# Window attention feeding a gated FFN: softplus dummies, other homes for gated parts, seven half products in ten chunks instead of eleven, fewer fillers, a new written-out order

## The chip, the cores and the metric

One core of one Trainium2 chip. The metric is device time in microseconds of one execution. The kernel before takes 897.61 us as the median of three runs (897.12 to 897.76). Engine names are those of the profile: PE (TensorE matmul), PEld (its weight load), DVE (VectorE), ACT (ScalarE), POOL (GpSimd), SP (the DMA-issuing queue).

## The reference, cut to what matters

Eight batches of eight heads, 576 positions, head width 64. Then 4608 tokens go through an FFN with d_model 512 and d_ff 2048.

```python
scores = scale * q @ k.T                       # only 0 <= i - j < 64 is kept
attn = exp(scores - rowmax) ; attn /= attn.sum + 1e-9
x = (attn @ v)  reshaped to (4608, 512)
h = x @ w_in
sp = max(h, 0) + log1p(exp(-abs(h)))           # softplus
g = h * erf(sp)
out = g @ w_out                                # float32
```

The weights come as 64-bit floats; the chip unpacks them. Each float32 operand of a product is scaled and split into two float16 parts (hi, lo), and a product is hi·hi + hi·lo + lo·hi, so every multiplication costs three matmuls.

## The kernel before, in words

The 4608 tokens are 36 attention units `u` of 128 tokens, and 18 FFN chunks `c` of 256 tokens. A chunk's FFN has two halves of d_ff, so there are 36 groups `g`; from chunk 2 on, group g belongs to chunk g // 2.

There is no planner on the chip. `PLAN` is one long string of tokens such as `sp:35:1`; the loop at the end of the kernel calls a handler for each token in that order, and each handler issues its instructions at once. Each engine therefore runs its own instructions strictly in the order in which their tokens stand, and waits with semaphores for data of the others. A last letter names the engine where there is a choice: a ACT, v DVE, g POOL, d a DMA that POOL issues.

The tokens that the change and the prediction touch:

- `wm:n` issues n filler matmuls on PE that nothing reads (line 993).
- Attention of a unit: `s` scores on PE (505), `m` masked maximum on DVE (514), `f` subtract it, `e` the exponential on ACT (539), `ph` and `r` its hi and lo parts (577/579 and 546), `a` the product with v, `n` the normalization.
- First FFN product, chunks 4 to 17 (from `FIRST`): `M:g:m`, seven products m = 1, 2, 6, 5, 7, 4, 3 of 24 matmuls with 128 columns each (809), into two PSUM banks; `E` copies a bank out and `C` (825, DVE) adds the other bank to what was copied, into the buffer `hb[g % 2]`.
- Activation: `sp:g:n` softplus on ACT (833), `er:g:n` erf on ACT (837), `gt:g:n` the gate h · erf on DVE (842 from chunk `FAST` on, else 844). Exp, softplus and erf are in different activation tables, so ACT loads a table (`ACT_TABLE_LOAD`) wherever the kind changes.
- Second FFN product, below `FAST`: `gh` and `gl` split the gate into hi and lo, `mA` and `mB` multiply by w_out in 512-column matmuls (868; 96 of them for a chunk), `fo` takes the result out.
- Second FFN product, from `FAST` on: seven half products in the order `SERIES` = 1, 4, 2, 5, 6, 3, 7 as listed by number, run as 1, 4, 2, 5, 6, 7, 3 in the plan. `A` and `B` (577/579 and 933) make the hi and lo part of one quarter of the gate, held in `yb`, and put them into a place that `slot(c, m, h)` names; `P` and `Q` (954) multiply them, in 256-column matmuls (168 for a chunk); `S` adds one quarter to another for the later products; `O` clears a PSUM bank; `K` and `J` (420/422 and 971/974) take results out. The combined right-hand sides come from w_out through `Z`, `Yh`, `Yl`.

`slot` in the kernel before puts two products' parts in halves of `hb[1]`, the buffer of the odd groups; only products 1 and 7 of the last chunk (`NCH` - 1 = 17) go into `vr`, the buffers of the attention's v, which are free by then. `E` of group 35 writes `hb[1]`, so in program order it stands behind all `P` and `Q` of chunk 16.

`FAST` also sets `LONE` (how many units have doubled attention buffers) and `LENT` (from which chunk the gate's split uses `hb`).

Of the kernel before, what the change touches and what calls it, by code (L numbers as in the profile page):

```python
# [18 lines left out]
B, H, S, D = 8, 8, 576, 64  # L19
# [25 lines left out]
FAST = 7  # L45
# [246 lines left out]
def window_attention_gated_ffn(ctx, tc, q, k, v, w_in, w_out, masks, out):  # L292
# [538 lines left out]

    def softplus(g, n):
        nc.scalar.activation(at(yb, g, n), at(hb, g, n), AF.Softplus, scale=st_c[g][:, n:n + 1])  # L833

    def erf(g, n):
        y = at(yb, g, n)
        nc.scalar.activation(y, y, AF.Erf)  # L837
# [228 lines left out]
```

## Time and profile before

| what | value |
|---|---|
| median of three runs | 897.61 us |
| the profiled execution's own time | 895.71 us |
| its span, first to last instruction | 893.8 us |
| PE busy | 821.5 us (92%) |
| DVE busy | 787.4 us (88%) |
| ACT busy | 702.4 us (79%) |
| POOL busy | 406.2 us (45%) |
| mean granted TensorE clock | 0.990 |

The profile is of one execution. Engine names with a trailing q are the engine's sequencer, which waits. "busy" is the union of the instructions' own times; a matmul's end is modelled, so matmul rates are better read from starts of uniform runs of matmuls. In a chain of waits, each piece is the work that the next piece waited for, from the last instruction backwards. Lines such as L954 are lines of the kernel before.

### The profile page before, as it was taken

To read this page: it belongs to the slowest core of one execution; us is meant where nothing else is said; L and a number is where in the kernel's file an instruction comes from. 1 tells how busy PE (TensorE), PEld (TensorE's weight loads), DVE (VectorE), ACT (ScalarE), POOL (GpSimd) and SP (SyncE) were. 2 spreads that over 40 slices of the span, in tenths; PEclk is the share of its full clock that TensorE was granted. 3 is DMA by queue.
4 is the path that set the end of the run, shared out by engine and by line. 5 is a ranking of instruction groups with operands and counts; after the bars stand their busy time and mean duration, and the time that the engine had idled before them with its cause. 6 is when DMAs were issued, how large, how long until landed. Compare 5 with 4: busy or idle time off the path is not lost.

```text
span 893.8 us, 28169 instructions
## 1 busy us (share of the span) xinstructions
PE 821.5 (92%) x11952; PEld 679.9 (76%) x11952; DVE 787.4 (88%) x1680; ACT 702.4 (79%) x960; POOL 406.2 (45%) x384
## 2 busy tenths in 40 slices
PE   7989998999999989999889999899899998999977
PEld 6878766576676646678788878788789887889866
DVE  5799999999999989999999989898889898777845
ACT  3799989799999886979698869886779865765662
POOL 3253464431553336556473737553635352542332
PEclk9999999999999999999999999999999999999999
DMA  9963366434647354534557776793675733422100
GB/s 360 397 210 128 120 168 136 106 103 83 134 98 149 87 135 100 134 104 108 121 125 162 132 134 133 139 192 84 137 115 127 109 76 63 90 49 69 25 25 24
DMA packets 149101, 111.52 MB, mean 125 GB/s; under 512 B 123504, under 2 KB 123888, under 8 KB 148976
## 3 DMA queue, kind: packets, MB, share of 16 engines
q1 hardware_dynamic: 145808, 98.60, 45.4%
q0 software_dynamic: 3024, 11.01, 6.8%
q8 instruction: 93, 1.52, 0.7%
q14 instruction: 32, 0.26, 0.1%
q10 hardware_dynamic: 144, 0.13, 0.0%
HBM read 59.64 MB, written 9.44 MB: 77 GB/s over the span
## 4 chain that ended last, share of the span: by engine, by line
DVE 41%; PE 26%; ACT 21%; issue 9%; DMA 3%; POOL 1%; SPq 0%; DVEq 0%; ACTq 0%; POOLq 0%
PE o L954 9%; PE hp L809 8%; DVE h L933 5%; ACT y L833 4%; DVE sm L514 4%; DVE y L842 3%; ACT y L837 3%; DVE h L825 3%; ACT h L577 2%; ACT L833 2%; PE o L868 2%; DVE vs L427 2%; PE hp L765 2%; PE av L993 2%; ACT L837 2%
## 5 line engine op out<-in xcount | busy, mean ns | idle before, releaser
L954 PEld LDWEIGHTS <-h 128*128 128x128 f16 x1800 | 172.1, 98 | 52.7 <-ACT h L577 11.8
L809 PE MATMUL hp<-arena,w 128*128 128x128 f16 x2688 | 163.8, 219 | 5.4 <-DVE h L825 3.0
L809 PEld LDWEIGHTS <-w 128*128 128x128 f16 x2688 | 155.5, 98 | 12.5 <-issue 7.0
L954 PE MATMUL o<-w,h 128*128 128x256 f16 x1008 | 124.7, 276 | 16.1 <-ACT h L577 9.5
L809 PE MATMUL hp<-arena 128*128 128x128 f16 x2016 | 122.3, 220 | 12.6 <-ACT h L577 8.4
L809 PEld LDWEIGHTS <-arena 128*128 128x128 f16 x2016 | 116.1, 98 | 18.4 <-issue 15.2
L933 DVE TENSOR_TENSOR h<-y,h 128x512 f16<-128x512 f32 x107 | 89.2, 856 | 11.2 <-ACT h L577 6.0
L933 POOL TENSOR_TENSOR h<-y,h 128x512 f16<-128x512 f32 x43 | 57.4, 1339 | 73.3 <-ACT h L577 36.3
L765 PE MATMUL hp<-arena,w 128*128 128x256 f16 (+1 forms) x960 | 88.8, 252 | 1.7 <-ACT h L577 1.0
L833 ACT ACTIVATE y<-h,c 128x1024 f32<-128x1024 f32 x72 | 80.6, 1143 | 9.4 <-DVE h L825 7.1
L577 ACT ACTIVATE h<-y 128x512 f16<-128x512 f32 x101 | 59.4, 620 | 34.6 <-PE o L954 17.3
L765 PEld LDWEIGHTS <-w 128*128 128x128 f16 x960 | 77.4, 98 | 11.2 <-issue 2.1
L577 ACT ACTIVATE h<-hp 128x512 f32<-128x512 f32 x111 | 64.5, 583 | 19.1 <-PE hp L809 16.7
L868 PE MATMUL o<-w,gh 128*128 128x512 f16 x320 | 75.1, 379 | 1.1 <-DVE ob L982 1.1
L837 ACT ACTIVATE y<-y 128x1024 f32<-128x1024 f32 x72 | 74.8, 1051 | 0.4
L842 DVE SCALAR_TENSOR_TENSOR y<-h,small,y 128x1024 f32<-128x1024 f32 x44 | 57.4, 1316 | 19.6 <-ACT y L837 19.5
L825 DVE TENSOR_TENSOR h<-hp,h 128x512 f32<-128x512 f32 x84 | 57.4, 684 | 13.5 <-PE hp L809 10.9
L954 PE MATMUL o<-spare,h 128*128 128x256 f16 x506 | 62.0, 273 | 6.9 <-DVE ob L974 3.5
L833 ACT ACT_TABLE_LOAD x39 | 50.0, 1283 | 22.9 <-DVE h L825 14.9
L514 DVE CUSTOM_DVE_ANT_0 sm<-s,mask 128x128 f32<-128x128 f32 x268 | 60.9, 284 | 6.2 <-PE s L505 4.2
L519 POOL TENSOR_TENSOR sm<-sm,small 128x512 f32<-128x512 f32 x42 | 51.7, 1236 | 28.7 <-DVE small L514 22.1
L868 PEld LDWEIGHTS <-gh 128*128 128x128 f16 x320 | 30.5, 98 | 33.8 <-issue 1.4
(254 smaller groups left out, 1743.7 us busy)
## 6 DMA issues: line engine op xcount, KB each, us to landing
vr<-v_in SPq DMA_DIRECT2D x36, 520.0 KB, 4.1
kr<-k_in SPq DMA_DIRECT2D x36, 384.0 KB, 4.0
y<-y POOLq DMA_DIRECT2D x21, 512.0 KB, 4.9
qr<-q_in SPq DMA_DIRECT2D x36, 256.0 KB, 3.4
out<-ob SPq DMA_DIRECT2D x33, 256.0 KB, 2.4
arena<-w_in SPq DMA_DIRECT2D x4, 1024.0 KB, 8.6
w<-w_in SPq DMA_DIRECT2D x4, 1024.0 KB, 8.8
arena<-w_out SPq DMA_DIRECT2D x4, 1024.0 KB, 5.4
```

The costliest lines, as they stand in the source:

```text
L514: nc.vector.tensor_tensor_reduce(smi(u, par)[:, j, :], sps[par][:, j, :], mask[:, var, :], 1.0, LOWEST, op0=ALU.add, op1=ALU.max, accum_ou ...
L519: eng_of(eng).tensor_tensor(s, s, m.unsqueeze(2).broadcast_to([P, HP, P]), op=ALU.subtract)
L577: nc.scalar.activation(dst, src, AF.Copy)
L765: nc.tensor.matmul(hps[pc % 2][:, f, at_t], w1[a][hf][:, cc, fs], xt[b][c % 2][:, cc:2 * NCC:NCC, :][:, at_x, :], start=(n == 0), stop=(n ...
L809: nc.tensor.matmul(bank[:, q, f, :], left(m, a, 2 * hf + q)[:, cc, f * P:(f + 1) * P], xt[b][c % 2][:, slot + cc, :], start=m in (1, 2, 5) ...
L825: nc.vector.tensor_tensor(dst, bank_view(1), dst, op=ALU.add)
L833: nc.scalar.activation(at(yb, g, n), at(hb, g, n), AF.Softplus, scale=st_c[g][:, n:n + 1])
L837: nc.scalar.activation(y, y, AF.Erf)
L842: nc.vector.scalar_tensor_tensor(y, at(hb, g, n), gain(g, n), y, op0=ALU.mult, op1=ALU.mult)
L868: nc.tensor.matmul(ops[j], a[:, f // 2, j, f % 2, :], w2[b][:, hf * GF + n * GF // 2 + f, :], start=n == 0 and f == 0 and a is gh and b == ...
L933: eng_of(eng).tensor_tensor(lo, quadrant(m)[:, 512 * h:512 * (h + 1)], hi, op=ALU.subtract)
L954: nc.tensor.matmul(dst, a[:, at_f], right(m, n, 2 * h + f // 2)[:, f % 2], start=False, stop=f == 3 and (a is lo or n == 1), skip_group_ch ...
```

## The change

- `FAST` goes from 7 to 8: chunk 7 uses the plain second product, ten chunks (8 to 17) use the half products. `LONE` goes from 4 to 5, `LENT` from 5 to 6.
- `preload` is new: an activation of one column with scale 0, whose only effect is that ACT has the table of its function. The plan has 36 such dummies, `tl:g`, all softplus (`tx`, for exp, is not used).
- `slot`: the parts of chunk 16 go into `vr`, those of products 1 and 7 of chunk 17 into `qr` and `kr`; the rest stays.
- Fillers: 18 `wm` tokens with 350 matmuls become 16 with 165.
- The order of the whole plan is another, with some instructions on other engines. Token counts by engine: `E` on DVE 29 to 36, `K` on DVE 9 to 17, `r` on DVE 29 to 36, `gl` 28 to 32, `B` on DVE 108 to 100; `A` on ACT 102 to 90, `K` on ACT 24 to 13, `E` on ACT 83 to 76, `gh` on ACT 24 to 29; `B` on POOL 46 to 40, `r` on POOL 31 to 24, `gn` on POOL 15 to 8; `mA` and `mB` 56 to 64 each, `P` and `Q` 154 to 140 each.

```diff
-FAST = 7
+FAST = 8
...
     shift14 = few(1)
+    warm = few(1)
...
+    def preload(n, kind):
+        nc.scalar.activation(warm, shift14, {"s": AF.Softplus, "x": AF.Exp}[kind], scale=0.0)
...
     def slot(c, m, h):
         i = SERIES.index(m)
-        if c == NCH - 1 and m in (1, 7):
-            t = vr[0 if m == 1 else 1].rearrange("p a b c -> p (a b c)")[:, 512 * h:512 * (h + 1)]
+        if c == NCH - 2:
+            t = vr[i % 2].rearrange("p a b c -> p (a b c)")[:, 512 * h:512 * (h + 1)]
+        elif c == NCH - 1 and m in (1, 7):
+            t = (qr if m == 1 else kr)[h].rearrange("p a b -> p (a b)")[:, :512]
         else:
             k = 512 * (i % 2) + 1024 * h
             t = hb[1][:, k:k + 512]
```

The handler table gains `"tl": lambda g: preload(g, "s")`. Of the plan, the start, one place with dummies, and the end:

```diff
-    "lv:1 lk:0 lq:0 lm lq:1 lk:1 lv:0 L:0 pk:1:2:v wm:41 s:0 m:0:1 lk:2 lq:2 L:1 m:0:0 f:0:1:g wm:48 s:1 f:0:0:g pk:0:2:a "
...
-    "L:4 lk:5 lq:5 xh:1:a d:9 wm:65 s:4 b:2:a l:1 lq:6 c:9 wm:8 mb:1 m:4:0 L:5 tp:3:0 a:2:0 mx:1 e:3:0 f:4:0:g xl:1:v my:1 "
...
-    "st:16:0 O:17:1 M:35:6 gt:34:1 M:35:2 E:35:1:a A:17:1:0:a M:35:7 B:17:1:0:g C:35:0 A:17:1:1:v M:35:5 E:35:2:a "
-    "B:17:1:1:v S:17:7:g M:35:4 C:35:1 M:35:3 E:35:3:a A:17:7:1:g P:17:1:0 C:35:2 B:17:7:1:g Q:17:1:1 sp:35:1 P:17:1:1 "
-    "A:17:7:0:g sp:35:0 Q:17:1:0 B:17:7:0:g er:35:0 er:35:1 gt:35:0 gt:35:1 A:17:2:0:a P:17:2:0 A:17:4:0:v A:17:4:1:a "
...
+    "lq:0 lk:0 lm lv:0 lv:1 lq:1 lk:1 L:0 wm:15 s:0 m:0:0 lk:2 lq:2 m:0:1 L:1 pk:0:2:a f:0:0:g L:3 f:0:1:g wm:19 tp:0:0 "
...
+    "M:24:1 yt:13:0:1 C:23:2 tl:27 sp:23:1 M:24:2 pk:31:2:v sp:23:0 pa:15 E:24:0:v pb:15 px:15 M:24:6 C:24:0 er:23:0 py:15 "
...
+    "A:16:3:0:a M:35:5 gt:34:1 E:35:2:a er:34:0 B:16:3:0:g M:35:4 C:35:1 gt:34:0 M:35:3 tl:35 A:17:1:1:g E:35:3:v "
+    "A:17:1:0:a Q:16:3:1 B:17:1:1:g C:35:2 Q:16:7:1 P:16:7:1 sp:35:1 B:17:1:0:v S:17:7:v Q:16:7:0 sp:35:0 P:16:7:0 "
+    "A:17:7:1:g Q:16:3:0 J:16:2 P:16:3:0 O:17:0 Q:17:1:1 er:35:0 P:17:1:1 er:35:1 gt:35:0 P:17:1:0 P:16:3:1 gt:35:1 "
+    "A:17:2:0:a P:17:2:0 J:16:1 A:17:4:1:a A:17:4:0:g st:16:0 Q:17:1:0 B:17:2:0:v A:17:2:1:a st:16:1 O:17:1 P:17:4:1 "
...
```

## Rows read from the trace of the kernel before

**Rows 1.** The page, busy time of each engine over the span.
```profile
PE 821.5 (92%) x11952; PEld 679.9 (76%) x11952; DVE 787.4 (88%) x1680; ACT 702.4 (79%) x960; POOL 406.2 (45%) x384
```
**Rows 2.** Five stretches: length, busy of PE, PEld, DVE, ACT, POOL (count), clock, DMA.
```profile
0.00:60.00 60.00, 50.38 (x876) 45.95 (x878) 43.95 (x160) 39.19 (x56) 20.45 (x37) 0.97 0.89 341
60.00:450.00 390.00, 367.76 (x4892) 267.30 (x4887) 370.85 (x802) 343.46 (x478) 181.48 (x155) 0.99 0.50 118
450.00:700.00 250.00, 229.31 (x3826) 208.13 (x3826) 227.95 (x498) 204.86 (x284) 132.53 (x127) 1.00 0.68 136
700.00:860.00 160.00, 150.59 (x2143) 138.35 (x2141) 129.03 (x203) 102.59 (x128) 59.88 (x57) 0.99 0.34 65
860.00:894.00 34.00, 23.46 (x231) 20.16 (x228) 15.57 (x20) 12.35 (x17) 11.88 (x10) 0.95 0.05 16
```
**Rows 3.** Waits of DVE, 60 to 450 us, longest group (us in total, times, longest).
```profile
DVE cmx L453 <- ACT junk L445: 3.2, 3, 1.8
```
**Rows 4.** Waits of DVE, 0 to 60 us, those for PE's scores.
```profile
DVE sm L514 <- PE s L505: 3.4, 2, 2.1
DVE spare L514 <- PE s L505: 3.2, 3, 1.9
```
**Rows 5.** Chain of waits, 835 to 894 us: start us, us, what.
```profile
855.41 8.07 PE hp L809 x144
...
863.51 0.70 DVE h L825
...
864.28 1.28 ACT L833
...
865.57 2.19 ACT y L833 x2
...
867.78 1.28 ACT L837
...
869.07 1.07 ACT y L837
...
870.16 1.30 DVE y L842
...
871.48 0.64 ACT h L577
...
872.16 10.23 PE o L954 x80
```
**Rows 6.** Chain of waits of the whole span, its shares by line.
```profile
by line: PE o L954 8.8%; issue 8.6%; PE hp L809 7.9%; DVE h L933 4.8%; ACT y L833 4.4%; DVE sm L514 3.5%; DVE y L842 3.4%; ACT y L837 2.8%; DVE h L825 2.7%; ACT h L577 2.4%; ACT L833 2.4%; PE o L868 2.4%; DVE vs L427 2.0%; PE hp L765 1.6%; 
```
**Rows 7.** Chain of waits, one uniform run of 512-column matmuls.
```profile
339.85 6.04 PE o L868 x28
```
**Rows 8.** DVE groups by line, whole span: busy us, mean ns, idle before.
```profile
L933 DVE TENSOR_TENSOR h<-y,h 128x512 f16<-128x512 f32 x107 | 89.2, 856 | 11.2 <-ACT h L577 6.0 <-ACT y L833 2.4 <-POOL h L579 1.0
L825 DVE TENSOR_TENSOR h<-hp,h 128x512 f32<-128x512 f32 x84 | 57.4, 684 | 13.5 <-PE hp L809 10.9 <-ACT h L577 2.3
L427 DVE SCALAR_TENSOR_TENSOR gl<-y,small,gh 128x1024 f16<-128x1024 f32 x20 | 27.4, 1372 | 0.4 <-ACT gh L420 0.4
```
**Rows 9.** Chain of waits, 0 to 60 us, the fillers.
```profile
7.26 2.71 PE av L993 x48
...
33.02 3.53 PE av L993 x65
```
**Rows 10.** ACT groups by line, whole span.
```profile
L577 ACT ACTIVATE h<-y 128x512 f16<-128x512 f32 x101 | 59.4, 620 | 34.6 <-PE o L954 17.3 <-DVE y L940 8.9 <-DVE y L842 4.6
L833 ACT ACT_TABLE_LOAD x39 | 50.0, 1283 | 22.9 <-DVE h L825 14.9 <-issue 4.5 <-DVE h L933 1.6
L399 ACT ACTIVATE small<-small 128x1 f32<-128x1 f32 x1 | 0.2, 203 | 0.0
```
**Rows 11.** PE in order of time, 872 to 876 us, two runs of eight matmuls.
```profile
872.16 1.89 PE L954 MATMUL o<-w,h 128*128 128x256 f16 x8 [6.07 <-ACT h L577]
...
875.23 1.04 PE L954 MATMUL o<-w,h 128*128 128x256 f16 x8
```

More of the change, by code (lines that the diff above doesn't have):

```diff
@@ L1003, in window_attention_gated_ffn @@
         "W": w_in_scale, "V": w_out_scale, "X": joint_scale, "dc": descale, "gn": gains, "mm": mm1, "ev": hidden,
-        "sp": softplus, "er": erf, "gt": gate, "gh": g_hi, "gl": g_lo, "mA": lambda g, n, j: mm2(g, n, j, 0),
+        "sp": softplus, "tl": lambda g: preload(g, "s"), "tx": lambda u: preload(u, "x"), "er": erf, "gt": gate, "gh": g_hi, "gl": g_lo, "mA": lambda g, n, j: mm2(g, n, j, 0),
         "sz": last_store,
```

450 rows, old and new, of the table PLAN are left out of this document.

## The prediction

> **What bounds the kernel now.** I read the page's busy times first, then stretches, then who waits in each stretch, then the chain of waits. PE is busy 92% and DVE 88% of the span [rows 1]; no engine alone sets the time. By stretches [rows 2] there are four regimes. Up to 60 us PE is busy 50.4 of 60 us, much of it fillers, DVE 44.0, and the DMA engines 0.89: the start waits for data. From 60 to 450 us DVE is busy 370.9 of 390 us (95%), and its longest group of waits there is 3.2 us [rows 3]: DVE is the engine that sets the pace. From 450 to 700 us PE (92%) and DVE (91%) are both nearly full and trade short waits. From 700 us the attention runs out, DVE falls to 81%, PE has 94%. The last 34 us have PE at 23.5 us: there a chain is open. It is in the chain of waits [rows 5]: the last first-product matmuls end at about 863.5, then join (863.51), table load (864.28, 1.28 us), two softplus, table load, erf, gate (870.16), hi part (871.48), and only at 872.16 the next half product. PE had 2.6 us of work to put under that chain (24 matmuls of product 1 of chunk 17) and then stood for 6.07 us [rows 11].
>
> **The change part by part.** The sum is made against the profiled execution, 895.71 us (span 893.8 us and 1.9 us around it); the median, 897.61 us, is 1.9 us above it, and I add that at the end.
>
> *Chunk 7 goes over to the plain product.* It loses 168 matmuls of 256 columns and gets 96 of 512. In uniform runs one takes 8.07/144 = 56 ns at 128 columns and 6.04/28 = 216 ns at 512 [rows 5, 7]; between them by columns, about 109 ns at 256 (1.04 us for eight, the last of which ends late, agrees [rows 11]). So 96 · 0.216 = 20.7 against 168 · 0.109 = 18.3 us: PE +2.4 us. On DVE that chunk loses some ten `B` of 0.856 us and gets four `gl` of 1.372 us [rows 8]: about -3 us, in a stretch where DVE sets the pace. Ends: -3 and +2.4. I take +2, near PE's, since over the whole plan DVE gets back what it loses here (next).
>
> *Instructions on other engines.* DVE gets 7 `E` and 8 `K` (nearest row the join, 0.684 us: +10.3), 7 `r` (nearest row `B`, same shapes, 0.856: +6.0), 4 `gl` (+5.5); it loses 8 `B` (-6.8) and, priced each by the mean of its own kind, some twenty others (3 `S`, 3 `J`, peaks, `T`, scalings) against a few small additions, about -13. Net +2 us on 787. ACT loses 12 `A` of 0.62 us, 11 `K`, 7 `E` [rows 10] and gets 5 `gh`: about -10 us before the dummies. POOL loses about 12 us. I count the +2 of DVE together with the +2 of PE above as one term of +2, because where one of them sets the pace the other has room; ends 0 and +5.
>
> *The new order in the middle.* Summing instructions in both plans with these durations up to the softplus of group 28 (724 us before), DVE has 7 us more to do by then and PE 3 us less; after that point PE has 140 us of work instead of 145. If DVE's 7 us count at its busy share (91%), +6.4, less 4.7 us of PE work that is no longer behind it: +2 us. In between, the distances in PE work from each product to the reader of its result are alike (from a chunk's last `M` to its first product of the odd half about 11 us of PE work before, 10 after). Ends -6 and +8: the two engines' common idle time in 450 to 700 us is about 20 us each, and I don't see how a third of it could move more than that.
>
> *Fillers.* 185 fewer, 3.53/65 = 54 ns each [rows 9]: 10 us of PE, all in the first 100 us. Four of their runs lie on the chain in the first 60 us (48, 31, 22 and 65 matmuls, 10.1 us; the first and last are shown). But the start waits for DMA, so not all of it comes back. What is seen to wait for PE there is DVE for scores that stand behind fillers: 3.4 + 3.2 = 6.6 us [rows 4]. Of that the share of fillers removed, 185/350, gives -3.5 us. Ends 0 (the data are late anyway) and -10; on the other side +8, if the clock falls (a rival below).
>
> *Dummies.* The number of table loads stays (39 for softplus before and after; the 36 dummies cause most of them). A dummy helps only if it stands ahead of a softplus whose data are still to come; by the order of ACT's tokens that is so at 11 of the 36 (groups 17 to 21, 23, 25, 27, 29, 31, 35); the others stand beside a softplus that has the table already, and in three places an exp comes between, so that the load is wasted (3.8 us of ACT, which has a fifth of its time free). Before, the loads stood idle 22.9 us, mostly for the join: they came after the wait [rows 10]. On the chain they have 2.4% of the span, 21 us, 16 loads [rows 6]; six of the groups with a useful dummy are among them, and group 35. Six times 1.283 is 7.7 us; I take -3, because between 450 and 800 us a second path through DVE or PE is mostly about as long. Each dummy costs 0.2 us of ACT [rows 10], 7 us in all, covered by the 10 us that ACT loses. Ends 0 and -7.7. The Trainium skill (ScalarE: Activation LUTs, What ACT_TABLE_LOAD costs) gives a switch of tables as a load of 1283 ns and a drain of 1380 ns, 2.66 us. The load agrees; of the drain these rows show nothing: the load at 867.78 follows the softplus that ends at 867.76, and erf starts 0.01 us after the load [rows 5]. By the page the six would be worth 16 us and this term -6; the trace decides.
>
> *The end.* Chunk 16's parts go to `vr`, so `hb[1]` is free and group 35's products stand between chunk 16's. After the last `M:35` six `P` and five `Q` now come before the first product that needs group 35's gate: 68 matmuls · 0.109 = 7.4 us of PE work. The chain from there was 872.16 - 863.5 = 8.7 us; `tl:35` takes its first load out: 7.4 us. So the wait of 6.07 us goes to about zero: -6.0. After it the eight first matmuls took 1.89 us instead of 1.04 [rows 11], at a granted clock of 0.95 in this stretch, so at the lower of the two levels for some 2.4 us: without the wait another -1. Together -7. The price: POOL's DMA sum for product 3 of chunk 17 (`S:17:3:d`) instead of DVE's, some 6 us of latency with about 7 us of products to hide under, and the chunk's 16 products in front of group 35's on PE's queue, whose `A` and `B` come from three engines; if one is late, the `M` behind it is too. Ends 0 and -8.
>
> Sum: 895.7 + 2 + 2 - 3.5 - 3 - 7 = 886.2; with the 1.9 us up to the median, **888 us**.
>
> **The rivals.**
>
> *All of it counts:* the fillers -6.6, the dummies -7.7, the order 0: 895.7 + 2 - 6.6 - 7.7 - 7 + 1.9 = 878 us. For it: the chain's 21 us of loads and 10 us of fillers. Against: DVE is full from 60 to 450 us, and what is early there waits for it.
>
> *Nothing is left:* fillers 0 (data), dummies 0 (second path), the end -4 (the sum by DMA late): 897.6 + 4 - 4 = 897.6 us. For it: the start's DMA share; against: the 6 us hole is plain.
>
> *Slower, DVE becomes the bound of the fast chunks:* 22 instructions of `E`, `K` and `r` move onto it, 16.3 us, mostly behind 450 us, while most of what it loses is chunk 7's and the attention's. DVE has 22 us free from 450 to 700 us [rows 2], but in pieces that wait for ACT and PE. If four fifths of the 16.3 us stay (13 us), and only the end's -7 stands against it, with half of the fillers: 897.6 + 13 - 7 - 1.7 = 902 us. It decides from the point where DVE has under 3% idle in that stretch. Against it: the tally, +2 over the whole span.
>
> *Slower, the clock in the start:* fillers hold PE's activity while it waits for data. Before, the clock of the first 60 us was 0.97 [rows 2]; after one wait of 6 us the matmuls ran at half speed [rows 11]. If a third of the real PE work in the first 50 us (some 22 us, its tokens counted at their uniform durations) runs at the lower level, it takes 7 us more, and 8 with DVE behind it: 888 + 3.5 + 8 = 899 us. The Trainium skill (TensorE: Matmul & The Clock Gate, HAM oscillation) has the same from another kernel: PE that waits for DMA between short bursts is put back to the lower clock at each wait. Against it: PE is not the last to arrive in the start, and 165 fillers stay.
>
> **How the numbers follow.** Chances: the forecast (881 to 894) 0.55; all counts 0.14; nothing left 0.11; DVE bound 0.14; clock 0.06. A measurement tells 0.2% from no change, that is 895.8 to 899.4. Faster: 0.55 + 0.14 = 0.69. Within: 0.07 of the third case and 0.01 of the last, 0.08. Slower: 0.04 + 0.14 + 0.05 = 0.23. The range 877 to 901 takes in the forecast, nearly all of the first and third rival and half of the slower ones; some 2 in 10 lie outside. The likeliest case alone is 881 to 894.
>
> **What would show it.** End: after the last `M:35` PE waits under 1 us before product 2 of chunk 17, and the clock of the last 34 us is 1.0. Dummies: loads before softplus idle less than 10 us in all, and their share of the chain falls from 2.4% to under 2%. Fillers: DVE's wait for scores in the first 60 us falls to about 3 us, clock not below 0.95. Method: 64 `mA` of eight matmuls; DVE busy about 789 us. Wrong: DVE busy over 95% from 450 to 700 us, or PE waits of more than 2 us between chunk 16's half products and group 35's, or a start with a clock of 0.9.

## The result and the profile after

The changed kernel takes 866.94 us (865.29 to 869.73), beside 897.37 us (896.8 to 897.76) for the kernel before on the same chip: ratio 0.9665, 95% interval 0.9638 to 0.9692. That is -30 us; the forecast was -9.6 us and a range down to 877 us. The direction was right, the size wrong by a factor of three. The profiled execution has a span of 864.4 us. In what follows a difference in us is a ratio times 897.4 us, so that runs of different groups can be set side by side.

Busy times, the page of the changed kernel:

```profile
PE 809.7 (94%) x11693; PEld 659.1 (76%) x11693; DVE 787.9 (91%) x1685; ACT 701.0 (81%) x976; POOL 403.4 (47%) x371
```

DVE does what it did before to half a microsecond [rows 1], and the tally of the forecast said so. So the whole gain is time in which DVE no longer stands idle: 106 us before, 76 us now. Where, by stretches (length, busy of PE, PEld, DVE, ACT, POOL, clock, DMA share, GB/s):

```profile
0.00:60.00 60.00, 46.68 (x744) 40.83 (x745) 46.04 (x164) 41.86 (x67) 21.09 (x38) 0.97 0.92 354
60.00:450.00 390.00, 374.07 (x4940) 265.38 (x4938) 373.86 (x804) 346.60 (x477) 192.94 (x157) 1.00 0.52 119
450.00:700.00 250.00, 232.56 (x3867) 208.90 (x3865) 238.05 (x513) 211.81 (x315) 123.28 (x115) 1.00 0.68 136
700.00:830.00 130.00, 126.56 (x1835) 117.50 (x1834) 106.47 (x178) 84.72 (x99) 53.42 (x51) 1.00 0.27 54
830.00:864.00 34.00, 29.80 (x320) 26.50 (x317) 23.51 (x30) 16.03 (x22) 12.71 (x11) 0.98 0.17 47
```

Against [rows 2], DVE's idle time falls by 2 us up to 60 us, by 3 from 60 to 450, by 10 from 450 to 700 (22.1 to 12.0), and by 15 behind 700 (49.2 to 34.4). The stretches that DVE paces gave almost nothing; those in which PE, ACT and DVE wait for each other gave nearly all. These are stretches of time and not of work: at the end of group 18's products the changed kernel is already 14.7 us ahead (the ladder below), of which DVE's idle time up to 450 us explains 5; the rest is work of DVE that the new order does later.

What DVE waited for there is the gate's wait for ACT. DVE's waits over the whole span, the kernel before (us in total, times, longest):

```profile
DVE y L842 <- ACT y L837: 19.5, 13, 6.0
```

It was DVE's longest group of waits, 13 times up to 6.0 us, and the forecast did not look at it: [rows 3] end at 450 us. The changed kernel:

```profile
DVE y L845 <- ACT y L840: 6.3, 8, 1.7
...
DVE y L847 <- ACT y L840: 1.5, 2, 0.8
```

ACT's groups for softplus in the changed kernel (busy us, mean ns, idle before); L836 is the dummy:

```profile
L833 ACT ACT_TABLE_LOAD x25 | 32.1, 1283 | 5.1 <-DVE h L825 4.7
...
L836 ACT ACT_TABLE_LOAD x14 | 18.0, 1283 | 0.2
```

Of 36 dummies 14 hold a load; the others find the table there. The loads are 39 as before, but ACT idles 5.3 us ahead of them in place of 22.9 [rows 10]. On the chain of waits, loads ahead of softplus had 2.4% [rows 6]; now they are not among its fourteen largest rows, so under 1.7%, and PE's first product leads:

```profile
by line: PE hp L809 13.7%; PE o L959 9.8%; PE o L871 7.8%; issue 7.4%; DVE h L938 3.9%; DVE y L845 2.6%; DVE sm L514 2.5%; DVE y L847 2.4%; ACT y L833 2.1%; PE hp L765 2.0%; DVE w L427 2.0%; DVE h L825 2.0%; DVE h L579 1.7%; DVE gl L427 1.7
```

The end, chain of waits 815 to 862 us (start us, us, what), the part that answers to [rows 5]:

```profile
835.99 0.61 DVE h L825
...
836.68 2.19 ACT y L833 x2
...
838.87 0.02 issue
838.88 1.28 ACT L840
840.17 0.01 issue
840.18 1.06 ACT y L840
...
841.27 2.48 DVE y L845 x2
...
846.89 4.98 PE o L959 x44
```

The first load is gone; from join to gate the chain is as long as its instructions. PE meanwhile works: in 836 to 847 us it is busy 10.49 of 11 us.

```profile
836.00:847.00 11.00, 10.49 (x97) 9.01 (x95) 8.89 (x12) 7.78 (x10) 1.64 (x3) 1.00 0.13 48
847.00:861.00 14.00, 13.31 (x120) 11.54 (x118) 8.89 (x13) 2.93 (x5) 5.90 (x5) 1.00 0.28 67
```

PE's longest wait there for a part of the gate, from 835 us on, is 0.4 us, where the kernel before had the hole of 6.07 us [rows 11]; the clock behind it is 1.00. (The 0.98 of the stretch from 830 us comes from its last 4 us, by the end of PE's work at 860.9 us.)

```profile
PE o L959 <- DVE h L938: 0.4, 1, 0.4
```

### The profile page after: what moved, and what is told of

Same layout as the page of the kernel before. It is cut to its first block, busy times and chain, and to the rows that moved or that the text cites. A ratio compares the mean times of both kernels' runs of the same rounds, so it can differ in the third digit from the quotient of the medians.

```text
span 864.4 us, 27620 instructions
## 1 busy us (share of the span) xinstructions
PE 809.7 (94%) x11693; PEld 659.1 (76%) x11693; DVE 787.9 (91%) x1685; ACT 701.0 (81%) x976; POOL 403.4 (47%) x371
## 4 chain that ended last, share of the span: by engine, by line
DVE 38%; PE 37%; ACT 12%; issue 7%; DMA 3%; POOL 2%; SPq 0%; DVEq 0%; ACTq 0%; POOLq 0%
PE hp L809 14%; PE o L959 10%; PE o L871 8%; DVE h L938 4%; DVE y L845 3%; DVE sm L514 3%; DVE y L847 2%; ACT y L833 2%; PE hp L765 2%; DVE w L427 2%; DVE h L825 2%; DVE h L579 2%; DVE gl L427 2%; ACT h L577 2%; DVE vs L427 1%
## 5 line engine op out<-in xcount | busy, mean ns | idle before, releaser
L959 PEld LDWEIGHTS <-h 128*128 128x128 f16 x1464 | 138.1, 98 | 39.1 <-DVE h L938 11.2
L959 PE MATMUL o<-w,h 128*128 128x256 f16 x816 | 99.8, 273 | 4.3 <-DVE h L938 3.0
L871 PE MATMUL o<-w,gh 128*128 128x512 f16 x384 | 89.6, 379 | 0.2 <-DVE arena L987 0.2
L938 DVE TENSOR_TENSOR h<-y,h 128x512 f16<-128x512 f32 x92 | 77.7, 870 | 3.1 <-ACT y L833 1.2
L577 ACT ACTIVATE h<-y 128x512 f16<-128x512 f32 x81 | 48.3, 620 | 32.6 <-PE o L959 14.6
L871 PEld LDWEIGHTS <-gh 128*128 128x128 f16 x384 | 36.4, 98 | 39.7 <-issue 0.7
L959 PE MATMUL o<-spare,h 128*128 128x256 f16 x414 | 51.6, 273 | 7.7 <-DVE h L938 4.2
L845 DVE SCALAR_TENSOR_TENSOR y<-h,small,y 128x1024 f32<-128x1024 f32 x40 | 52.7, 1334 | 6.6 <-ACT y L840 6.3
L938 POOL TENSOR_TENSOR h<-y,h 128x512 f16<-128x512 f32 x30 | 38.6, 1294 | 34.6 <-ACT h L577 15.6
L539 ACT ACTIVATE sm<-sm,small,cde 128x512 f32<-128x512 f32 x58 | 46.3, 808 | 5.5 <-POOL sm L519 4.3
```

The lines of the kernel that those rows point to most:

```text
L577: nc.scalar.activation(dst, src, AF.Copy)
L845: nc.vector.scalar_tensor_tensor(y, at(hb, g, n), gain(g, n), y, op0=ALU.mult, op1=ALU.mult)
L871: nc.tensor.matmul(ops[j], a[:, f // 2, j, f % 2, :], w2[b][:, hf * GF + n * GF // 2 + f, :], start=n == 0 and f == 0 and a is gh and b == ...
L938: eng_of(eng).tensor_tensor(lo, quadrant(m)[:, 512 * h:512 * (h + 1)], hi, op=ALU.subtract)
L959: nc.tensor.matmul(dst, a[:, at_f], right(m, n, 2 * h + f // 2)[:, f % 2], start=False, stop=f == 3 and (a is lo or n == 1), skip_group_ch ...
```

## The experiments

**Theory:** the dummies are the largest part. A table load that starts only when the join is done delays the gate by 1.28 us, DVE waits for that gate with nothing else in its order, and this repeats from group to group. **Rivals:** the new order by itself; the end; the fillers; the seventh plain chunk.

**no_dummies.** The changed kernel without its dummies.

```diff
-    "M:24:1 yt:13:0:1 C:23:2 tl:27 sp:23:1 M:24:2 ..."
+    "M:24:1 yt:13:0:1 C:23:2 sp:23:1 M:24:2 ..."
...
```

> The changed kernel without its 36 softplus dummies, all else as in the changed kernel (867 us). Theory order (the new order of instructions on all engines carries the 30 us, the dummies little): 868 to 870 us, that is at most 3 us lost, and softplus loads that wait for the join come back in the trace. Theory dummies (table loads out of the chain carry much of the 30 us): 875 us or more.

Measured: 880.06 us, ratio 0.9804 (0.978 to 0.9829), +12.5 us against the changed kernel. Its loads idle as in the kernel before, and DVE waits for erf again (L834), 19.1 us in the two kinds of gate together in place of 7.8:

```profile
L827 ACT ACT_TABLE_LOAD x36 | 46.2, 1283 | 22.4 <-DVE h L819 21.9
```
```profile
DVE y L839 <- ACT y L834: 17.6, 12, 3.0
...
DVE y L841 <- ACT y L834: 1.5, 2, 0.8
```

Of the 14 loads in dummies three were not needed: without dummies 36 loads are left of 39. The other eleven, 14.1 us, stand behind the wait for the join again, and 12.5 us of that is in the time. The chain of waits of this kernel shows where. Its shares by line, and two of its pieces:

```profile
by line: PE hp L803 12.3%; PE o L953 9.5%; issue 8.4%; PE o L865 7.7%; DVE h L932 3.8%; DVE y L839 3.0%; ACT y L827 2.6%; DVE y L841 2.4%; DVE sm L508 2.3%; DVE h L819 2.1%; DVE w L421 2.0%; PE hp L759 1.9%; ACT y L834 1.8%; ACT L827 1.8%; 
```
```profile
451.34 1.28 ACT L827
...
849.22 1.28 ACT L827
```

There are twelve such pieces, 15.4 us: the loads ahead of the softplus of groups 17 to 21, 23, 25, 27, 29, 31 and 35, all eleven that the forecast called useful, and that of group 14, which is on the chain of the changed kernel too.

**before_dummies.** The other side: the kernel before, with a dummy ahead of the first softplus after each table change (39), nothing else.

```diff
-    ... lv:24 C:17:2 sp:17:1 gt:16:0 a:22:1 ...
+    ... lv:24 C:17:2 tl:17 sp:17:1 gt:16:0 a:22:1 ...
...
```

> The kernel before (897.4 us) with nothing changed but 39 softplus dummies, one ahead of the first softplus after each change of table. Theory dummies (the load then runs while ACT waits for the join; without the dummies the changed kernel lost 13 us): 885 to 890 us, idle before softplus loads down from 22.9 us to about 5. Rival, the forecast's: a second path is as long in the old order, so 893 to 897 us.

Measured: 883.02 us, ratio 0.9855 (0.9832 to 0.9877), -13.0 us. The loads (now L835) are still there and idle 0.7 us; DVE's wait for erf halves:

```profile
L835 ACT ACT_TABLE_LOAD x39 | 50.0, 1283 | 0.7
...
L835 ACT ACTIVATE small<-small 128x1 f32<-128x1 f32 x39 | 7.9, 203 | 0.4
```
```profile
DVE y L844 <- ACT y L839: 10.2, 10, 4.7
```

DVE's wait falls by 9.3 us and the time by 13.0. Part of the difference goes with PE's clock. Around 335 us PE in the kernel before waits 3.46 us, and the four matmuls behind it take 1.89 us; with the dummies PE waits 2.30 us there and the four take 1.04. From 335 to 340 us the granted clock is 0.66 before and 1.00 with the dummies (before first, then before_dummies):

```profile
335.44 0.23 PE L457 MATMUL av<-ident,cmx 128*128 128x128 bf16 x1 [3.46 <-DVE cmx L412]
336.04 1.89 PE L868 MATMUL o<-w,h 128*128 128x512 f16 x4 [0.37 <-ACT h L577]
...
335.00:340.00 5.00, 4.20 (x32) 2.85 (x33) 4.10 (x10) 2.37 (x4) 1.66 (x3) 0.66 0.21 43
```
```profile
333.54 0.23 PE L456 MATMUL av<-ident,cmx 128*128 128x128 bf16 x1 [2.30 <-DVE cmx L411]
334.14 1.04 PE L870 MATMUL o<-w,h 128*128 128x512 f16 x4 [0.37 <-ACT h L576]
...
335.00:340.00 5.00, 5.00 (x43) 3.03 (x42) 4.97 (x8) 4.13 (x6) 4.41 (x3) 1.00 0.74 95
```

A part of the change that can be made without its order brings 43% of its gain. This settles the first point: the forecast's -3 is refuted from both sides.

**dummies_each.** The changed kernel with one dummy ahead of every first softplus after a table change, and no other.

```diff
-    tl in 36 places of the plan, 14 of which cause a load
+    tl in 36 places, each ahead of the first sp after an er or an e
```

> The changed kernel with its 36 dummies put elsewhere: exactly one ahead of the first softplus after each table change, so that all loads before a softplus stand in a dummy, none in the softplus itself. In the changed kernel 14 of 36 dummies held a load and 25 loads stood before a softplus, idle 5.1 us in sum. If these 5 us lie on the chain: 862 to 864. If a dummy that loads nothing (0.2 us each, 22 of them) is what costs: 863 to 865. If the remaining loads lie beside other work: 866 to 868.

Measured: 867.14 us, ratio 0.9667 (0.9643 to 0.9692): the same as the changed kernel. All loads before a softplus are now in dummies:

```profile
L832 ACT ACT_TABLE_LOAD x36 | 46.2, 1283 | 0.6
```

The 5 us that were left idle lie beside other work, and 22 dummies without a load cost nothing that can be seen. No better version here.

**before_tail.** The kernel before with only the new end and the new homes.

```diff
-    the plan of before from M:33:1 on; chunk 16's parts in hb[1]
+    the plan of after from M:33:1 on without tl; chunk 16's parts in vr
```

> The kernel before with one part of the change: from the first half product of group 33 on it follows the new order with the new homes and the new engines of the gated activations; no dummies, all 350-odd fillers, all ten half-product chunks. By the forecast's end term (the hole of 6.07 us and 1 us of clock, minus nothing else) 889 to 891 us against 897. The rival from the old-tail run (13 us lost when the old tail is put into the changed kernel): 884. A seam between two orders that costs more than the tail gives: 895 or more. In the profile TensorE's wait behind the last gated activations falls from 6 us to under 1 if the theory of the end holds.

Measured: 891.22 us, ratio 0.994 (0.992 to 0.996), -5.4 us; the forecast's term was -7 (with the dummy of group 35 in it). PE's longest wait for the gate's parts in the end falls from 6.1 to 1.4 us, not under 1 as expected. Before and in this kernel:

```profile
PE o L954 <- ACT h L577: 6.1, 1, 6.1
```
```profile
PE o L956 <- ACT h L574: 1.4, 1, 1.4
```

**old_tail** and **old_tail_new_homes.** The changed kernel with the end of before, with the old and with the new homes.

```diff
-    the plan of after from M:33:2 on
+    what is left then, in the order and on the engines of before
```

> The changed kernel up to the start of group 33's products, then everything that is left in the order, with the engines and with the homes of the kernel before. Theory end (as forecast, the wait of 6 us and its half clock): 873 to 876 us, with a PE wait of about 6 us before product 2 of chunk 17. Theory middle (the gain lies in the stages before, the end adds little because something else is late there): 869 us or less.

> The changed kernel with the order of before from group 33's start on, but with the new homes of the last gated activations (the old-tail run had the old homes too, 879.9 us). If a home by itself only matters where the order uses it: 879 to 881, as the old tail. If the homes alone relax the waits of the gated activations for their buffers: 874 to 877. The whole new tail gives 867.

Measured: 879.86 us, ratio 0.98 (0.9776 to 0.9823), and 878.62 us, ratio 0.9792 (0.9767 to 0.9816): +12 and +11 us. The hole is back in both (6.2 us in the second); in the first:

```profile
PE o L953 <- ACT h L573: 6.1, 1, 6.1
```

The intervals overlap: homes alone give nothing that can be measured; they only allow the order. The 12 us are more than the 5.4 us of before_tail; two orders that don't belong together meet at group 33, both kernels also lack `tl:35` (13 loads in dummies, not 14), and what of the 12 us is the seam and what the dummy these runs don't separate.

**before_165.** The kernel before with 165 fillers.

```diff
-    ... pk:1:2:v wm:41 s:0 ... f:0:1:g wm:48 s:1 ... d:9 wm:65 s:4 ...
+    ... pk:1:2:v wm:19 s:0 ... f:0:1:g wm:23 s:1 ... d:9 wm:31 s:4 ...
...
```

> The kernel before with its 350 fillers cut to 165, each group by the same share, nothing else. Forecast's term: -3.5 us (894). The changed kernel lost 2.5 us when it got 349 fillers, so 895 by the sum of parts. If nothing is early in the start because DVE sets the pace from 60 us on: 0 (897). If the clock of the start falls: 900 or more, with a granted clock under 0.95 in the first 60 us.

Measured: 894.84 us, ratio 0.9979 (0.9968 to 0.9991), -1.9 us.

**fillers_350** and **no_fillers.** The changed kernel with 349 fillers, and with none.

```diff
-    16 wm tokens, 165 matmuls
+    fillers_350: the same 16 tokens, 349 matmuls
+    no_fillers: no wm token
```

> The changed kernel with each of its filler runs made 2.1 times as long, 349 fillers in all instead of 165. Forecast's term: 870 to 872 us (3.5 us more). Rival, the start waits for data and DVE: 866 to 868 us. Rival, fillers stand wholly in the way: 876 us.

> The changed kernel with no fillers at all (165 taken out). By the slope of 349 to 165 (2.5 us for 184): 864.5, below both kernels. If what is left of the fillers lies beside waiting for data: 866 to 868. If the fillers that remain hold the clock: 870 or more, with a granted clock under 0.95 in the first 60 us and matmuls there at about 110 ns for 128 columns in place of 56.

Measured: 869.51 us, ratio 0.9696 (0.9673 to 0.9718), and 865.91 us, ratio 0.9669 (0.9647 to 0.9691), where the changed kernel has 0.9665. The intervals of all three overlap: 349 fillers cost 2.8 us as measured, and taking out the last 165 gives nothing that can be told. The first 60 us show what changes: with 349, with 165 (above) and with none, the granted clock is 1.00, 0.97 and 0.89, DVE's busy time 44.2, 46.0 and 45.0 us. Of these only the 0.89 stands clear: old_tail, with the same start as the changed kernel, has 0.94, and before_tail, with the start of before, 1.00 where before has 0.97.

```profile
0.00:60.00 60.00, 49.61 (x884) 44.70 (x885) 44.23 (x160) 41.33 (x65) 20.40 (x38) 1.00 0.90 343
```
```profile
0.00:60.00 60.00, 42.78 (x588) 35.34 (x589) 44.95 (x161) 41.49 (x66) 20.97 (x38) 0.89 0.90 338
```

And in the chain of no_fillers the first two runs of scores, 32 matmuls (L500), take 1.98 and 1.92 us. In the changed kernel (L505) the first run takes 1.98 us as well, the second 1.04: in no_fillers PE has waited for the data and still runs at the lower of its two levels, 1.2 GHz.

```profile
3.55 7.61 DMA kr<-k_in
11.29 1.98 PE s L500 x32
...
16.53 1.92 PE s L500 x32
```
```profile
4.74 1.98 PE s L505 x32
...
9.86 0.59 PE av L998 x11
11.20 1.04 PE s L505 x32
```

In these 60 us no_fillers has 156 matmuls fewer, by 54 ns each [rows 9] an estimate of 8.4 us, and PE is busy only 3.9 us less: slower matmuls take part of it again. That this is why the time stays is argued, not shown.

**before_dummies_165** and **before_three.** Parts put together on the kernel before: dummies and fewer fillers; then the end and the homes as well. What is then left of the change is the new order, the engines and chunk 7 in the start and the middle.

```diff
+    before_dummies_165: tl as in before_dummies, wm as in before_165
+    before_three: that, and from M:33:1 on as in before_tail
```

> The kernel before with both the 39 dummies (alone -13.5 us, 883) and the cut to 165 fillers. With the old end; before_three had the new end on top and came to 873.4. If the fillers are worth 2.5 us here too: 880.5, and the new end 7 us. If the new end is worth 5.4 us with the dummies as without: 878.8, and the fillers 4.2 us. If fillers are worth nothing in the old order: 883, and the new end 9.6 us once the dummies are in.

> The kernel before with three parts of the change and without its new order in the start and the middle: a dummy softplus ahead of the first softplus after each table change, about 165 fillers in place of 350, and the new tail with the new homes from group 33 on. If the parts add up: 897 - 13.5 (dummies) - 2.5 (fillers) - 7 (end) = 874 us. If the new order and the seventh chunk are worth nothing in themselves, 867, as the changed kernel. If the dummies and the tail take the same time twice (their waits overlap): 880 or more.

Measured: 878.56 us, ratio 0.9802 (0.9779 to 0.9826), -17.8 us; and 873.41 us, ratio 0.9733 (0.9707 to 0.9759), -24.0 us. Alone the three give -13.0, -1.9 and -5.4, in sum -20.3; together a few us more, at the edge of the intervals. One on top of the other they give -13.0, -4.8 and -6.2. Start and middle are left with 0.9733 to 0.9665, -6 us, by the two intervals somewhere from -3 to -9.

**old_start.** The changed kernel with before's order up to the first product of group 8, with 350 fillers.

```diff
-    the plan of after up to M:8:1
+    the plan of before up to M:8:1, then what is left of after's
```

> The changed kernel, but everything up to group 8's first product (some 235 us, with the 350 fillers) in the order and with the engines of the kernel before. Theory fillers and start (10 us of fillers off PE, about 3.5 us expected): 870 to 872 us. Rival, the start is bound by data and DVE, so its order and fillers cost nothing: 866 to 868 us. If the start is better in the old order: under 865 us.

Measured: 873.75 us, ratio 0.9737 (0.9714 to 0.976), +6.5 us, of which 2.8 are the fillers (fillers_350). Group 8's products end at 258.3 us here, later than in either order (248.6 and 251.1), so a seam is in this number too.

**old_middle** and **old_middle_dummies.** The changed kernel with before's order and engines from group 18 to group 33, without and with dummies there.

```diff
-    the plan of after from M:18:1 to M:33:1
+    what is left then, as in before (second kernel: with a tl ahead
+    of each first sp after a table change)
```

> The changed kernel, but from group 18's first product to group 33's first product (chunks 9 to 16, about 470 to 790 us) in the order and with the engines of the kernel before; start and end as in the changed kernel. Theory order in the middle: 874 to 880 us, DVE and PE idle 8 us more in that stretch. Rival, the middle is worth nothing and what is seen there is carried over from the stages before: 866 to 869 us.

> The changed kernel with the order and engines of before from the first product of group 18 to that of group 33 (as in the old-middle run, 890.8 us), but with a dummy ahead of the first softplus after each table change there too, which the old-middle run lacked. If the old middle lost its 24 us by the missing dummies (about 8 of the 13 that dummies are worth) and 16 are the order: 882. If the new order of the middle is worth only what the sum of parts leaves it (867 against 873.4, 6.5 us for start and middle): 872 to 874. If the old middle's loss is a seam between orders: above 884.

Measured: 890.77 us, ratio 0.9928 (0.9907 to 0.995), and 882.97 us, ratio 0.9852 (0.9835 to 0.987): +24 and +17 us. Dummies are 7 of the 24. The other 17 are more than the 6 us that start and middle have to give together. The trace shows where they arise: the products of group 18 end at 484.5 us in the second kernel and at 467.0 in the changed one, with the same order up to the seam. There 22 tokens, 12 of them combined right-hand sides (`Z`, `Yh`, `Yl`) that the new order had put off and the old had done by then, now come ahead of the first product; from 460 to 470 us PE is busy 2.72 of 10 us.

**method_alone.** The kernel before with chunk 7 by the plain product, in the old order; some 10 tokens had to move.

```diff
-FAST = 7
+FAST = 8
...
-    A, B, P, Q, S, K, J, O of chunk 7
+    gh, gl, mA, mB, fo of groups 14 and 15 in their places
     (LONE and LENT kept at 4 and 5)
```

> The order, engines, homes and 350 fillers of the kernel before, no dummies, only chunk 7's second product by the plain method (with what this forces: some of chunks 6 and 7's plain products and the first combined right-hand side of product 7 moved a few tokens). Forecast's term: 898 to 901 us (+2). Rival, DVE sets the pace there and loses 3 us of work: 892 to 896 us.

Measured: 905.84 us, ratio 1.0106 (1.0085 to 1.0127), +9.5 us. Group 14's products end 2 us later than in the kernel before, group 17's 14 us: the loss is where chunk 7's work was put by hand. Put into the old order like this it costs time; its price in the new order was not measured.

**old_engines.** The changed kernel's order, with before's engine for each token that both have (506 differ).

```diff
-    ... E:24:1:v ...   (after's last letters)
+    ... E:24:1:a ...   (before's, wherever the token exists there)
...
```

> The changed kernel's order, dummies, homes and fillers, but each instruction that both kernels can put on ACT, DVE or POOL on the engine that the kernel before uses for it (506 tokens differ). Theory engines (the choice of engine, token by token, carries a good part of the 30 us, though the tally by engine hardly moves): 880 us or more. Rival, only the tally counts: 866 to 871 us.

Measured: 979.65 us, ratio 1.0939 (1.0908 to 1.0971), 9% over the kernel before. An order and its engines are one thing; the tally by engine can't be priced apart from it.

The ladder, from the traces, one execution of each kernel (us at which the last first-product matmul of a group ends, and the last instruction):

| kernel | group 8 | 18 | 24 | 30 | 35 | end |
|---|---|---|---|---|---|---|
| before | 248.6 | 481.7 | 625.7 | 770.1 | 863.5 | 890.8 |
| before_165 | 249.0 | 481.5 | 624.6 | 767.6 | 861.0 | 888.3 |
| before_dummies | 248.9 | 477.1 | 616.9 | 760.5 | 851.6 | 879.0 |
| before_dummies_165 | 249.0 | 477.3 | 617.1 | 756.4 | 847.2 | 873.6 |
| before_three | 249.0 | 477.5 | 617.5 | 756.8 | 844.4 | 870.8 |
| after | 251.1 | 467.0 | 610.8 | 741.9 | 835.7 | 861.4 |

## Why the forecast was wrong

**Dummies, the step that failed.** The forecast counted well: 11 useful dummies and 3 with a load that is then lost, 14 loads; the trace has 14. The price failed, at the sentence "Six times 1.283 is 7.7 us; I take -3, because between 450 and 800 us a second path through DVE or PE is mostly about as long." The runs show -13.0 us for 39 dummies in the old order and -12.5 us in the new one for eleven useful loads, group 35's among them, which the forecast had put into its end: 1.1 us for each. Two errors are in that step. First, the loads were looked up on the chain of the wrong order. The chain of before has seven of the eleven groups (19, 21, 23, 25, 29, 31, 35), as the forecast read it; but the dummies stand in the new order, and the chain of that order without dummies has all eleven (no_dummies). Eleven useful loads times 1.283 us, 14.1 us with group 35's, was the end to keep in the range, not 7.7. Second, "a second path" was assumed and not looked up, and it took over half of the term. The runs give back 12.5 of the 14.1 us in the new order, and 13.0 of the 21 us of loads on the chain in the old one. A sign was there: DVE, busy 88% [rows 1], waited 19.5 us for ACT's erf, more than for anything else. With the dummies alone that falls to 10.2 us, and taking the dummies out of the changed kernel raises it from 7.8 to 19.1 us, by 11.3 us where the time rises by 12.5. By the ladder the gain comes bit by bit from group to group: 4.6 us at group 18, 8.8 at 24, 9.6 at 30, 11.9 at 35.

The Trainium skill (ScalarE: Activation LUTs, What ACT_TABLE_LOAD costs) has a load of 1283 ns and a drain of 1380 ns at each switch. The load agrees in every run. Of the drain the trace of after shows nothing either: the load at 838.88 follows the softplus after 0.02 us, and erf starts 0.01 us behind the load.

**Order, engines and chunk 7: +4 forecast, -6 left.** The step was "If DVE's 7 us count at its busy share (91%), +6.4, less 4.7 us of PE work that is no longer behind it: +2 us", and +2 for the method. The tally of work was right: DVE is busy 787.9 us, "about 789" forecast. But a tally of work prices no waits, and waits are what changed: from 450 to 700 us DVE idles 10 us less, in a place for which the forecast saw no way "how a third of it could move more than that"; nearly half went, part of it by the dummies. In before_dummies DVE is busy 233.20 us in this stretch, in before_three 234.69, in after 238.05:

```profile
450.00:700.00 250.00, 235.06 (x3923) 213.85 (x3921) 233.20 (x506) 211.23 (x307) 135.79 (x128) 1.00 0.73 141
```
```profile
450.00:700.00 250.00, 236.27 (x3934) 214.73 (x3932) 234.69 (x508) 211.80 (x308) 134.52 (x128) 1.00 0.70 142
```

```profile
450.00:700.00 250.00, 224.89 (x3757) 201.27 (x3755) 230.51 (x496) 199.41 (x281) 120.18 (x112) 0.99 0.66 131
```

The third row is no_dummies. So some 5 to 7.5 of the 10 us came with the dummies and some 2.5 to 5 with the order, if the same 250 us of two kernels may be set side by side. One part of it was not in the forecast's sum at all, the clock outside the start and the end. In slices of 10 us the trace of before has a granted clock of 0.83 to 0.95 at 130 to 150, 330 and 740 to 760 us; the trace of after has 1.00 from 60 to 860 us. The missing shares of these slices add up to an estimate of 5 us of PE's time. No run separates it from the waits ahead of it. How the 6 us divide between order, engines and method stays open: each splice of two orders brought a seam as large as what it was to measure.

**The end: right.** The hole went as worked out, PE's wait from 6.07 to 0.4 us, clock 1.00 behind it. Forecast -7, measured -5.4 alone (where a wait of 1.4 us is left) and -6 on top of dummies and fillers. The price that was feared, POOL's DMA sum late, does not show in PE's waits.

**Fillers: near in size, wrong in its mechanism.** Forecast -3.5; -1.9 in the old order, -4.8 there on top of the dummies, -2.8 in the new, the last within intervals that overlap. But DVE's wait for scores in the first 60 us, which was to fall from 6.6 to about 3 us, did not:

```profile
DVE sm L514 <- PE s L505: 6.7, 1, 6.7
...
DVE spare L514 <- PE s L505: 1.1, 1, 1.1
```

In before_165 it did not fall either (7.4 us in the first 60). And in the old order nothing is early at group 18 (481.7 and 481.5 us); the gain appears at group 24 and behind. In the new order it is there from the start: with 349 fillers group 8 ends at 254.0 us, and at 250.8 to 252.6 in the four traces with the start of after. Why the old order shows it so late is open. With the dummies the two traces are 4.1 us apart at group 30, and about half of that arises between 750 and 760 us: there the granted clock of before_dummies falls to 0.83, behind a wait of PE of 2.16 us, and that of before_dummies_165 stays at 1.00, behind one of 1.75 us. So about half of it goes with a fall of the clock in one execution.

**The rivals.** *All of it counts* (878) had the right idea for the dummies and stopped at its 7.7 us. *DVE becomes the bound:* the sign it named, DVE over 95% from 450 to 700 us, did come (238.05 of 250 us, 95.2%), and the time fell all the same. An engine that does the same work in less time is fuller; the sign says nothing unless its work has grown. *Nothing is left* fell with the dummies and the end. *The clock in the start:* with 165 fillers it stayed at 0.97, in another trace of the same start at 0.94. With none it falls to 0.89 and the second run of scores takes nearly twice as long, so the mechanism is real; its price of 8 us is not seen. The Trainium skill (TensorE: Matmul & The Clock Gate, HAM oscillation) says that PE is put back to the lower clock when it waits for DMA between short bursts; no_fillers agrees in the clock, with no loss in the time (865.91 us).

## What to carry to other kernels

Price what a change takes away on the chain of waits of the order in which it will stand: here the chain of the old order had seven of the eleven loads, that of the new order all of them. Where the new order cannot be traced ahead, the full count belongs in the range. Look also at what an engine that is nearly full waits for over the whole span and what ends that wait; here that group was 19.5 us before, and the dummies gave 13.0. A table load that comes behind a wait for data is worth moving ahead of it, by a dummy activation of 0.2 us, even where the order stays as it is. Price a new order by its waits, not by the sum of its instructions, and don't expect to measure it by splicing two orders: here the seam cost as much.

## What was not expected of the hardware

Between 165 and no fillers the clock of the first 60 us goes from 0.97 to 0.89 and the second run of 32 score matmuls from 1.04 to 1.92 us, and the kernel takes the same time (866.94 and 865.91 us): in this kernel's start, which waits for data, the lower clock cost nothing that could be measured. In the middle it did cost: behind PE's wait of 3.46 us at 332 us, the clock was 0.66 for 5 us and four matmuls took 1.89 us in place of 1.04.
